# Three-slot units, more dynamic slots at the end, and a band made from a skewed slice, in a convolution with a mixture of experts

## The chip, the cores and the metric

The kernel runs on one core of a Trainium2 chip. A core has five engines with queues of their own: TensorE (PE; its weight loads are shown as PEld), VectorE (DVE), ScalarE (ACT), GpSimd (POOL) and SyncE (SP, which here only issues DMAs). The time is device microseconds of one execution. The kernel before was run 14 times: median 721.24 us, lowest 711.25, highest 727.46. The profile is of one execution of 717.46 us, whose span (first to last instruction) is 715.7 us.

## What is computed

First a depthwise convolution over time with 8 heads, each with 7 taps that went through a softmax; then a mixture of 8 experts with one expert for each token (top 1), in which the expert's output is scaled by the softmax gate and by a sigmoid gate.

```
x: (8, 3584, 192); weight: (8, 7); w_gate, w_output_gate: (192, 8); w1: (8, 192, 1024); w2: (8, 1024, 192)
w = softmax(weight); x_pad = 6 zero rows ahead of each sequence
conv[b, s, h, g] = sum_k w[h, k] * x_pad[b, s + k, h, g]
x = conv.reshape(28672, 192)
logits = x @ w_gate; e_idx = argmax(logits); gate_w = softmax(logits)[e_idx]
eom = sigmoid(x @ w_output_gate)
for e in range(8):
    mask = e_idx == e
    h = relu(x[mask] @ w1[e]); ye = h @ w2[e]
    out[mask] = gate_w[mask] * eom[mask, e] * ye
```

The scale by both gates is applied to the rows before the expert, which the relu lets through, since the scale is positive.

## The kernel before

**Units.** The 28672 tokens are cut into NU = 16 units of 1792 tokens: 16 blocks of BT = 112, a block on the partitions. Two sequences' halves make no difference to what follows, except that a unit at the start of a sequence has zero rows ahead.

**front_a(u)** (line 298, 16 steps, each ended by a `yield`): for each head one matmul pair with the band matrix (line 303) and an eviction into `cv`; then `load_x(u + 2)`; six transposes of `cv` into `tt` (line 317); the logits (line 326) into `lt`; a transpose back (line 335) into `gb`. Evictions go through `evac`, which sends them to ScalarE or VectorE (lines 291 and 293) by `evac_on` or in turn.

**front_b(u)** (line 347, 12 steps) is the routing. Step 1: largest logit and mask. Step 2: counts (line 374), gates. Step 3: four matmuls that give each token its place among those of its expert (lines 396 to 399). Step 4: the destinations `du` and the first permutation matrices `pm`. Steps 5 to 12: for each of eight groups of 224 tokens a permutation by matmul (line 457), eviction into `xs`, and a scatter of row pairs into the DRAM buffer `xcg`, which is sorted by expert (line 475, an indirect DMA of POOL, held in `pend` until `emit_in`). After the first group `plan(u)` computes on VectorE which rows the slots of this unit take: R counts the row pairs that an expert has received, DN those that slots have taken; a slot takes at most TP = 256 pairs (512 rows), and what is left stays for a later slot.

**Slots.** A `Slot` (line 608) is 512 rows of one expert. `slot_load` loads them with two DMA transposes (`xa`, `xb`, lines 586 and 588) and an index load (`xi`, line 590), all on SP; the loads of a unit wait until all its scatters have landed. `first(q2)` is half of the first layer with relu (lines 626 and 633; relu on ScalarE at 646, every fourth on VectorE at 644); `second(q)` is the second layer for 128 rows (line 668), evicted for two quarters together (line 674) into `y`; `emit_out` issues the indirect DMAs into the output (line 495, POOL). From unit U0 = 2 on each unit runs four slots, experts 0 to 3 in even units and 4 to 7 in odd ones; the last unit runs all eight, and then ND = 3 half slots of 256 rows whose expert is chosen at run time by `pick` (the expert with most left), with its weights copied by `w_dyn` into `wd`. A closing loop (line 803) takes full slots as long as rows are left; its count is 0 for these inputs.

**Order.** The order is written out by hand and nothing reorders it. Units 0 and 1 run their fronts first. Then, in the main loop (line 742), unit u has 16 positions, four for each slot (`pos = 4 * k + q`). While the slots of unit u run, the loop puts in between them the 16 steps of `front_a(u + 2)` as `fa`, the last eight steps of `front_b(u + 1)` as `fs` (its scatters, positions 0 to 7), and the first four steps of `front_b(u + 2)` as `fbn` (one at 12, one at 14, two at 15). After position 7 the loads of the next unit are issued (`loads(u + 1)`). `second` runs one slot behind `first`.

**Weights.** All experts' weights stay in SBUF (`wres`), loaded in 32 pieces by POOL: 8 before unit 0, 8 among units 0 and 1, 16 at positions 4 to 19 counted from unit 2.

**Setup.** The band matrix (118 x 112 for each head; one tap per diagonal) is made by VectorE with 14 predicated copies over four heads each (line 142). The gate weights `wg` are loaded on ScalarE's DMA queue, x tiles 0 and 1 on SP.

## Time and profile before

| | |
|---|---|
| median of 14 runs | 721.24 us (711.25 to 727.46) |
| profiled execution | 717.46 us, span 715.7 us |
| mean granted TensorE clock | 0.944 |
| first slot's first matmul | 78.10 us |
| one unit of four slots, from 380.37 to 423.07 | 42.70 us |
| last unit's first dynamic half slot starts | 687.15 us |
| output scatters on POOL | 246 x 994 ns |
| row scatters on POOL | 128 x 1040 ns |
| HBM read, written | 35.92 MB, 43.06 MB |

A profile line for an instruction gives its start in us from the start of the span, its length, engine, source line, operation, output and inputs, and in brackets how long the engine was idle before it and what released it. "issue" is idle time for which the profile shows no cause. Busy TensorE time is not TensorE at its peak; its clock is granted by a throttle and shown as a share of full speed.

### The profile page before, as it was taken

What the parts mean: (1) busy time and instruction counts of PE and PEld (TensorE: products, weight loads), DVE (VectorE), ACT (ScalarE), POOL (GpSimd) and SP (SyncE); (2) the same over time, 40 slices, a digit from 0 to 9 for tenths busy, and PEclk for the clock granted to TensorE, in tenths of its full rate; (3) what the DMA queues carried; (4) which work ended last, traced back from release to release, by engine and by line L of the source; (5) the groups of instructions that cost most, each with busy time, mean ns of one, the idle gap of its engine ahead of it and who ended that gap; (6) DMA issues with size and microseconds to landing.
All of it is one profiled execution on the core that took longest, in us unless ns stands there. A gap on an engine that the chain in (4) does not pass through costs nothing.

```text
span 715.7 us, 13578 instructions
## 1 busy us (share of the span) xinstructions
PE 609.9 (85%) x4544; PEld 368.8 (52%) x4544; DVE 380.0 (53%) x1310; ACT 377.3 (53%) x638; POOL 403.2 (56%) x419
## 2 busy tenths in 40 slices
PE   3998699869797989889799897997989798699883
PEld 1564265535554655546555554654555465365452
DVE  7666657428274573735639275472836539134121
ACT  2777466524654554545455554564555455455442
POOL 1487277746555565455555646565564645655563
PEclk9999899989999999989999999999999899899896
DMA  6989389945163462714536164462715234256310
GB/s 165 208 168 301 89 193 155 228 94 157 55 144 114 97 161 77 168 63 103 148 82 173 67 130 123 89 162 76 174 64 108 66 86 85 79 126 168 114 40 29
DMA packets 162568, 88.13 MB, mean 123 GB/s; under 512 B 116765, under 2 KB 153792, under 8 KB 162496
## 3 DMA queue, kind: packets, MB, share of 16 engines
q1 hardware_dynamic: 131872, 43.92, 27.7%
q0 software_dynamic: 29728, 43.30, 23.3%
q8 instruction: 36, 0.59, 0.3%
q14 instruction: 36, 0.29, 0.1%
q10 hardware_dynamic: 896, 0.03, 0.1%
HBM read 35.92 MB, written 43.06 MB: 110 GB/s over the span
## 4 chain that ended last, share of the span: by engine, by line
PE 64%; issue 11%; DVE 7%; ACT 6%; POOL 5%; DMA 4%; another core or an unknown queue 1%; POOLq 0%; SPq 0%; ACTq 0%; DVEq 0%
PE pyt L668 16%; PE pp L626 13%; PE pf L303 11%; PE pp L633 7%; PE pf L457 6%; PE pf L317 5%; POOL out_dram L495 4%; PE pf L326 4%; ACT ht L646 3%; DVE ht L644 2%; DMA out_dram<-y,oi 2%; ACT cv L291 1%; DVE band L142 1%; PE pf L335 1%
## 5 line engine op out<-in xcount | busy, mean ns | idle before, releaser
L495 POOL DMA_INDIRECT out_dram<-y,oi x246 | 244.5, 994 | 178.1 <-ACT y L674 115.7
L646 ACT ACTIVATE ht<-pp 128x1024 f16<-128x1024 f32 (+1 forms) x189 | 184.8, 1005 | 79.1 <-PE pp L633 36.4
L668 PE MATMUL pyt<-wres,ht 128*128 128x192 f16 x1920 | 194.5, 249 | 1.5 <-issue 1.5
L475 POOL DMA_INDIRECT xcg_sorted<-xs,du x128 | 133.1, 1040 | 110.3 <-ACT xs L291 69.4
L668 PEld LDWEIGHTS <-ht 128*128 128x128 f16 x1968 | 170.5, 99 | 27.6 <-issue 14.4
L303 PE MATMUL pf<-xt,band 118*112 118x384 f32 x256 | 111.0, 529 | 42.7 <-ACT cv L291 27.0
L644 DVE TENSOR_SCALAR ht<-pp 128x1024 f16<-128x1024 f32 (+1 forms) x63 | 75.4, 1197 | 111.3 <-PE pp L626 55.8
L626 PE MATMUL pp<-xa,wres 128*128 128x512 f16 x240 | 98.0, 408 | 12.8 <-ACT ht L646 9.6
L291 ACT CAST xs<-pf 128x388 f16<-128x388 f32 x128 | 62.0, 487 | 73.0 <-PE pf L457 40.1
L674 ACT COPY y<-pyt 128x384 f32<-128x384 f32 x123 | 59.1, 480 | 77.8 <-PE pyt L668 23.4
L626 PE MATMUL pp<-xb,wres 128*128 128x512 f16 x240 | 96.1, 401 | 0.7 <-DMA xb<-xcg_sorted 0.7
L633 PE MATMUL pp<-xb,wres 64*128 64x512 f16 x240 | 77.9, 403 | 0.5 <-ACT ht L646 0.5
L633 PE MATMUL pp<-xa,wres 64*128 64x512 f16 x240 | 78.0, 403 | 0.0
L457 PE MATMUL pf<-xrow,pm 112*128 112x194 f16 x512 | 67.8, 256 | 11.3 <-ACT xs L291 3.2
L626 PEld LDWEIGHTS <-wres 128*128 128x128 f16 x480 | 35.4, 100 | 79.0 <-issue 77.4
L303 PEld LDWEIGHTS pf<-xt,band 118*112 118x112 f32 x256 | 42.8, 188 | 61.5 <-ACT cv L291 29.8
L457 PEld LDWEIGHTS <-pm 112*128 112x128 f16 x512 | 47.0, 101 | 42.1 <-issue 20.9
L293 DVE COPY cv<-pf 112x384 f32<-112x384 f32 x48 | 26.4, 551 | 78.1 <-PE pf L303 72.8
L427 DVE TENSOR_SCALAR pm<-pos,pos 112x256 f16<-112x256 f16 x256 | 62.7, 305 | 0.0
L422 DVE TENSOR_TENSOR xrow<-cv,gs 112x384 f16<-112x384 f32 x121 | 61.9, 549 | 0.0
L317 PE MATMUL pf<-identf,cv 112*128 112x112 f32 x384 | 52.0, 262 | 9.3 <-DVE tt L293 4.4
L291 ACT COPY cv<-pf 112x384 f32<-112x384 f32 x80 | 38.0, 478 | 27.2 <-PE pf L303 21.0
(135 smaller groups left out, 435.9 us busy)
## 6 DMA issues: line engine op xcount, KB each, us to landing
xt<-in_x_dram SPq DMA_DIRECT2D x8, 1344.0 KB
xt<-in_x_dram SPq DMA_DIRECT2D x8, 1260.0 KB
out_dram<-y,oi POOLq DMA_INDIRECT x246
wres<-in_moe_w_dram POOLq DMA_DIRECT2D x8, 384.0 KB
wd<-wres SPq DMA_DIRECT2D x3, 768.0 KB
wres<-in_moe_w_dram POOLq DMA_DIRECT2D x8, 256.0 KB
xcg_sorted<-xs,du POOLq DMA_INDIRECT x128
xcg_sorted<-zrow SPq DMA_DIRECT2D x8, 256.0 KB
```

The costliest lines, as they stand in the source:

```text
L291: nc.scalar.copy(out=o, in_=i)
L303: nc.tensor.matmul(pc[0:BT, 0:NB * GH], band[0:KI, h, :], xt[0:KI, :, h * GH:(h + 1) * GH], start=True, stop=True)
L317: nc.tensor.matmul(pt[:, j * BT:(j + 1) * BT], cvf[0:BT, m * 2 * D + i * 128:m * 2 * D + (i + 1) * 128], identf[0:BT, 0:BT], is_transpose= ...
L427: nc.vector.tensor_scalar(out=pms[i][P, l, :], in0=pos16[P], scalar1=pos[P, l * NG + i:l * NG + i + 1], scalar2=None, op0=ALU.is_equal)
L457: nc.tensor.matmul(ps[:, r * XW:(r + 1) * XW], pm[P, l, r * 128:(r + 1) * 128], xr[P, l * NG + i, :], start=(r == 0 and l == 0), stop=(r = ...
L475: i = nc.gpsimd.indirect_dma_start(out=xcg2, out_offset=bass.IndirectOffsetOnAxis(ap=du[:, i:i + 1], axis=0), in_=xs.rearrange("p r w -> p ...
L495: i = nc.gpsimd.indirect_dma_start(out=out, out_offset=bass.IndirectOffsetOnAxis(ap=oi[:, j:j + 1], axis=0), in_=y[:, j, :], in_offset=Non ...
L626: nc.tensor.matmul(pps[r][:, l, :], w[:, o2:o2 + 128], x, start=(r == 0), stop=(r == 1))
L633: nc.tensor.matmul(pps[r][:, l, :], w[p0:p0 + 64, c:c + 128], x[p0:p0 + 64], start=(r == 1), stop=(r == 0))
L644: nc.vector.tensor_relu(out=ht, in_=pps[r])
L646: nc.scalar.activation(out=ht, in_=pps[r], func=AF.Relu)
L668: nc.tensor.matmul(self.pp[:, o:o + D], self.ht[fc // 2][:, fc % 2, q * 128:(q + 1) * 128], self.w[:, w:w + D], start=(fc == 0 and q % 2 = ...
```

## The change

Six edits, of which the first three belong together.

- Units 4, 6, 8, 10 and 12 run three slots instead of four (`THREE`). Experts are taken in a running order (`nexte`), so that a unit continues where the one before stopped; a run that passes expert 7 is planned in two parts. The last unit still runs all eight, in the running order.
- After the last unit there are six dynamic slots instead of three half ones: two full (512 rows) and four half (256 rows). Their weight copies use buffers of two pools in turn. The last slot of all evicts and scatters each quarter by itself (`end`).
- In the main loop the steps are laid out anew. Short units run `front_a` in 12 positions and only the first step of `fbn` (at 10); the unit after a short one, and unit 2, then run 11 steps of `fs` (positions 0 to 10) and issue the next loads after position 10 instead of 7. Other units run the four steps of `fbn` at 12, 13, 14 and 15. While a short unit scatters rows, `emit_out` holds back four output scatters; unit 14 holds back eight. Before the main loop only one step of `front_b(3)` is run instead of four.
- Weights: 12 pieces before unit 0, four in unit 0, 16 at positions 8 to 23.
- The band: tokens of a block are now in reversed order, so that each head's band is a skewed slice of one line of 229 numbers. Heads 0 and 1 are still made by predicated copies (7, over two heads each); the lines of heads 2 to 7 are written to DRAM by ScalarE's queue and read back with a step of one element per partition. The ids of the tokens (`idu`) follow the reversed order.
- The gate weights are loaded on SP, between x tiles 0 and 1. In unit 0 the transposes are evicted in turn by ScalarE and VectorE; before the main loop `lt` is evicted in two halves by both.

```diff
-    ND = 3
+    DYN = (TP, TP) + (TP // 2,) * 4
+    ND = len(DYN)
...
     xts = {0: load_x(0)}
+    for i, (p0, p1, d0) in enumerate([(0, 128, 0), (0, 64, 128), (64, 128, 0), (0, 128, 64)]):
+        nc.sync.dma_start(wg[p0:p1, i, 0:E], moe_w_gate[d0:d0 + p1 - p0, :])
+        nc.sync.dma_start(wg[p0:p1, i, E:2 * E], moe_w_output_gate[d0:d0 + p1 - p0, :])
     xts[1] = load_x(1)
...
+    HB = 2
+    LW = BT + KI - 1
     band = const.tile([128, H, BT], FP32)
-    nc.vector.memset(band, 0.0)
+    nc.vector.memset(band[:, 0:HB, :], 0.0)
+    wline = const.tile([1, H - HB, LW], FP32)
+    nc.vector.memset(wline, 0.0)
+    wldr = nc.dram_tensor("tap_lines", (H - HB, LW), FP32, kind="Internal").ap()
...
+    nc.scalar.copy(out=wline[:, :, BT - 1:KI], in_=cw[0:1, HB:H, :])
+    nc.scalar.dma_start(wldr, wline)
+    nc.scalar.dma_start(band[0:KI, HB:H, :],
+                        bass.AP(tensor=wldr.tensor, offset=wldr.offset,
+                                ap=[[1, KI], [LW, H - HB], [1, BT]]))
...
-    for h in (0, H // 2):
-        for k in range(KW):
+    for k in range(KW):
+        m = idpu[:, 128 - BT - k:128 - k]
...
+    load_w(12)
...
-    def emit_out():
-        while pout:
+    def emit_out(keep=0):
+        while len(pout) > keep:
...
+    THREE = (4, 6, 8, 10, 12)
+    nexte = [0]
     def plan(u):
         if u < U0:
             return []
-        p = plan_half(u % 2, "a")
-        if u == NU - 1:
-            p += plan_half((u + 1) % 2, "b")
+        n = 3 if u in THREE else 4 if u < NU - 1 else E
+        e0 = nexte[0]
+        nexte[0] = (e0 + n) % E
+        if n == E:
+            p = plan_run(0, E, "a")
+            return p[e0:] + p[:e0]
+        p = plan_run(e0, min(n, E - e0), "a")
+        if e0 + n > E:
+            p += plan_run(0, e0 + n - E, "b")
         return p
...
+            if self.end:
+                nc.scalar.copy(out=self.y[:, q, :], in_=self.pp[:, 0:D])
+                pout.append((self.y, self.oi, q))
...
-    drain(fbn, 4)
+    drain(fbn, 1)
...
+        late, short = u == U0 or u - 1 in THREE, u in THREE
+        last_s = 10 if late else 7
+        if short:
+            before = {0: 1, 2: 1, 4: 1, 6: 1, 8: 1}
+            after = {0: 1, 1: 1, 2: 1, 3: 1, 4: 1, 5: 1, 6: 1, 7: 1, 8: 1, 9: 1, 10: 1}
+        else:
+            before = {0: 1, 2: 1, 4: 1, 6: 1, 8: 1, 9: 1, 10: 1}
+            after = {1: 1, 3: 1, 5: 1, 7: 1, 8: 1, 9: 2, 10: 1, 11: 1}
...
-                if 0 <= 16 * (u - U0) + pos - 4 < 16:
+                if 0 <= 16 * (u - U0) + pos - 8 < 16:
                     load_w(1)
                 if q % 2 == 0:
                     s.first(q // 2)
-                if pos in (0, 2, 4, 6, 8, 10, 12):
-                    evac_on[0] = "act" if pos < 8 else None
-                    drain(fa, 1)
-                if pos == 14:
+                evac_on[0] = "act" if pos < 8 else None
+                drain(fa, before.get(pos, 0))
+                if late and pos == 2:
+                    drain(fs, 1)
+                if not short and pos in (14, 15):
                     drain(fbn, 1)
                 if prev is not None:
                     prev.second(q)
-                    emit_out()
+                    emit_out(8 if u == NU - 2 and pos < 8 else 4 if short and pos < 8 else 0)
...
-                if pos == 12:
-                    drain(fbn, 1)
-                if pos == 15:
-                    drain(fbn, 2)
-                if pos == 7 and u + 1 < NU:
+                if pos == 10 if short else pos in (12, 13):
+                    drain(fbn, 1)
+                if pos == last_s and u + 1 < NU:
                     nxt = loads(u + 1)
                 if u == NU - 1 and q == 3 and k < ND:
-                    todo.append(load_pick())
+                    todo.append(load_pick(DYN[k]))
```

## The prediction

> **What bounds the kernel now.** First the page's busy line and its slices: one engine is nearly full, and only TensorE.
>
> ```profile
> PE 609.9 (85%) x4544; PEld 368.8 (52%) x4544; DVE 380.0 (53%) x1310; ACT 377.3 (53%) x638; POOL 403.2 (56%) x419
> PE   3998699869797989889799897997989798699883
> ```
>
> Then the chain of waits inside one unit, in order of time (start, length, what). One slot's share of it:
>
> ```profile
> 410.75 0.43 PE pp L626 x2
> 411.18 0.54 PE pp L633 x4
> 411.72 0.54 PE pp L626 x2
> 412.64 0.66 PE pyt L668 x8
> ```
>
> The three first rows are half of a slot's first layer (1.51 us), the last is a quarter of its second layer. A full slot is 2 x 1.51 + 4 x 0.66 = 5.66 us of TensorE at full clock. The stretches say what a unit of four slots takes and how its idle time costs twice:
>
> ```profile
> 380.37:423.07 42.70, 38.19 (x292) 23.14 (x290) 24.43 (x80) 23.04 (x37) 23.84 (x24) 0.96 0.47 120
> 404.40:406.90 2.50, 2.50 (x9) 0.54 (x8) 0.00 (x0) 1.38 (x2) 1.89 (x3) 0.50 0.24 77
> 380.40:391.70 11.30, 9.93 (x74) 6.12 (x74) 10.78 (x43) 6.77 (x12) 6.05 (x7) 1.00 0.81 205
> ```
>
> Columns: stretch, length, busy of PE, PEld, DVE, ACT, POOL, granted clock, DMA share, GB/s. The unit from 380.37 to 423.07 has TensorE busy 38.2 of 42.7 us at a mean clock of 0.96. Its clock falls to 0.50 for 2.5 us after a gap. VectorE is full (10.8 of 11.3 us) only in the unit's first quarter. So the middle is TensorE's, and a slot taken away there is worth its TensorE time as long as rows arrive in time. The rows that tell when they do are these: the last row scatter of a unit, the first load that waits for it, and (from the first slot of all, where nothing else hides it) the time from load to matmul.
>
> ```profile
> 407.79 0.98 POOL L475 DMA_INDIRECT xcg_sorted<-xs,du  x1 [0.30 <-issue]
> 410.29 1.14 SPq L586 DMA_TRANSPOSE xa<-xcg_sorted  x1
> 411.62 1.15 SPq L588 DMA_TRANSPOSE xb<-xcg_sorted  x1
> 76.92 1.14 SPq L588 DMA_TRANSPOSE xb<-xcg_sorted  x1
> 79.42 0.59 PE L626 MATMUL pp<-xb,wres 128*128 128x512 f16 x1 [0.73 <-DMA xb<-xcg_sorted]
> ```
>
> Scatter to load 2.50 us, xa to xb issue 1.33 us, xb to its matmul 2.50 us: 6.3 us from the start of the last scatter until the next unit can run. Here the next unit starts at 423.07, 15.3 us after that scatter: 9 us to spare. The change spends this reserve.
>
> At the end there is no front work left; slots follow each other:
>
> ```profile
> 640.68 0.98 POOL L495 DMA_INDIRECT out_dram<-y,oi  x1 [2.02 <-ACT y L674]
> 647.41 0.98 POOL L495 DMA_INDIRECT out_dram<-y,oi  x1 [1.89 <-ACT y L674]
> 675.84 0.38 PE L626 MATMUL pp<-xa,wres 128*128 128x512 f16 x1
> 681.49 0.38 PE L626 MATMUL pp<-xa,wres 128*128 128x512 f16 x1
> ```
>
> Between the same row of two slots lie 6.73 us where they stall (647.41 - 640.68) and 5.65 where they don't. POOL's four output scatters take 4 x 1.29 = 5.2 us of it, so TensorE still leads.
>
> **Part by part. Slots removed.** Units 4, 6, 8, 10 and 12 run three slots: 5 slots less. Each is 5.66 / 0.96 = 5.9 us; bounds 5.65 (no stall goes with it) and 6.73 (the stalled tail row). 5 x 5.9 = -29.5 (-28.3 to -33.7).
>
> **Slots added at the end.** Three half dynamic slots become two full and four half: two full at 6.73 and one half more. Half slots start at 687.15 and 692.27 (5.1 us apart), and half of the next takes 2.19 us (692.27 to 694.46): 4.4 to 5.1, without stall 2 x 0.87 + 1.32 = 3.1. 13.5 + 4.4 = +17.9 (14.4 to 18.6). The extra picks are some fifteen VectorE instructions of about 0.2 us; three more is 9 us of VectorE, busy 8.9 of 30 us there, and five slots pass between a pick and its slot. The weight copies wd (768 KB, three more) ride SP: their issue follows every 5.5 us (653.94, 659.41), faster than a full slot is eaten. Both cost nothing; if the copies fell behind, each half slot would wait 5.5 - 4.4 = 1.1 us. The capacity of all slots, 55 x 256 + 2 x 256 + 4 x 128 = 15104 row pairs, stands against 14598 that the inputs fill, counted per unit and expert; nothing is left over, before or after, so the closing loop does not run.
>
> **Less reserve at unit ends.** Routing of the next unit is left over: after a short unit only its first step is done, so the scatters of the unit that follows end at position 10 instead of 7 (so too in unit 2). From there TensorE has until the next unit 5 x 0.66 + 2 x 1.51 + 0.44 (L335) + about 0.75 (L374 to L399) = 7.5 us. In the short units they end at position 7 of 12, with 2 x 1.51 + 4 x 0.66 + 2 x 0.38 (L317) + 1.64 (L326) + 0.44 = 8.5 us. What has to fit: 0.5 us (ACT's xs, 0.48), POOL's backlog (0 to 3 us; the scatter at 407.79 came 3.3 us after its matmuls, behind two output scatters) and 6.3: 6.8 to 9.8 us. The short units hold back four output scatters, which keeps their backlog low, and position 10 issues none of its own. A full backlog stalls 2.3 and 1.3 us, none stalls nothing. I take 0.4 us, nearer the low end, at 11 ends (five short, five after them, unit 2): +4.4 (0 to 20). What waits behind the loads on SP is the next input tile, now issued ahead of them in these units (some 7 us of transfer, started 8 us earlier; wanted a unit later).
>
> **Denser short units.** 16 front steps in 12 positions instead of 16. VectorE gets three more evictions of 0.55 in the first quarter, but loses the 2 us of routing that now lies at positions 13 to 15 of the unit before. I take 0; if not, it is inside the range above.
>
> **Routing spread out** in the other units (positions 12 to 15, one step each, instead of two at 15). In the unit shown TensorE idled 0.40 us at 383.76 and 0.97 at 391.36 for it. Seven such passages at 0.4: -2.8 (0 to -9.6).
>
> **Weights.** 12 instead of 8 pieces before the first unit; the last 16 four positions later, so eight instead of four fall on unit 3's scatters. Each piece holds POOL 0.6 to 0.96 us (with the gap 1.26). POOL is back to back from 131 to 149 there, its last scatter (146.62) 11.6 us behind its matmuls (135.0); 4 x 1.26 = 5 us more makes 16.6 + 6.3 = 22.9 against the 17.5 to 19 us a unit has left. Against it stands a wait of 8.19 us at 138.27, put down to an unknown queue in a stretch that moves 152 GB/s; it may go or stay. +1 (-8 to +5).
>
> **Prologue.** The first matmul waits for the band, not for x, whose transfer ends before 9 us:
>
> ```profile
> 10.89 0.45 PEld L303 LDWEIGHTS pf<-xt,band 118*112 118x112 f32 x2 [10.89 <-DVE band L142]
> 11.07 0.32 SPq L98 DMA_DIRECT2D xt<-in_x_dram  x1
> 9.00:10.00 1.00, 0.00 (x0) 0.00 (x0) 0.96 (x2) 0.00 (x0) 0.00 (x0) 1.00 0.13 4
> ```
>
> 14 predicated copies (9.5 us) become 7 of half the width (about 2.4). Heads 0 and 1 could start near 10.3, when x is known to have landed; heads 2 to 7 come through two DMAs in a row from 6.1 us on: two round trips of 2.5 to 4 give 11 to 14. The larger memset of the tap lines (1374 elements on one partition, against 896 in 0.81 us) ends before the taps land at 4.33, and the reversed order of tokens inside a block only changes constants. At most 2 us are won (15.59 is where the second four heads waited). But the gate weights now stand on SP ahead of x tile 1, the last behind the band's landing, so that tile's issue moves from 11.07 to 12 to 15, beside twelve weight pieces; it is wanted at 24.2 and took some 7 us alone, 13 if it shares. -0.5 (-2.5 to +3). The last slot evicts each quarter by itself: -0.5.
>
> Sum: -29.5 + 17.9 + 4.4 - 2.8 + 1 - 0.5 - 0.5 = -10.0 us on an execution of 717.46 us (span 715.7). That execution lies 3.8 below the median of 721.24; I take the difference off the median: 711.2 us.
>
> The Trainium skill, page "TensorE: Matmul & The Clock Gate", Part 1, speaks against the change: it says TensorE falls to half clock after an idle window of about 3.4 us and needs another such stretch of work to recover, so short reserves would be paid twice. The trace shows half clock (0.50) already after a gap of 2.40 us at 402.88, and full clock after 0.97. By the page's window stalls of 2.4 us would add nothing. By the trace, 2.4 us at each of 11 ends would add 11 x 1.6 us, and stalls of 0.4 us nothing.
>
> **Rivals.** (a) Forecast, rows arrive about in time: 711, own range 706 to 717. (b) Stalls leave with the slots (-33.7 + 16), routing pays -6, the unknown wait at 138 goes (-4): 721.2 - 27.7, with 4 for ends about 698. For it: TensorE idles 4.5 us a unit; against it: most of this is one ScalarE stall of about 3.6 us a unit, which the change doesn't touch. (c) The gain is used up: ends stall 1.3 us each (14.3 instead of 4.4), 721. For it: POOL's backlog of 3.3 us in the unit shown; against it, the held-back outputs. (d) Slower: the rows come late at all 11 ends by the full 2.3 us of POOL backlog, and the gap drops the clock (2.5 us at 0.50 and 1.5 at 0.76 lose 1.6 us): 11 x 3.9 = 43 instead of 4.4, 750; with the stall alone, 25, 732. It decides from (10.0 + 4.4) / 11 = 1.3 us an end. For it: reserves of 7.5 and 8.5 against needs up to 9.8; against it, the bounds need the worst queue every time. (e) The closing loop runs: each pass would add a load, a weight copy and a slot in series, 15 us or more; the count of rows excludes it.
>
> **Numbers.** (a) 0.52, (b) 0.20, (c) 0.14, (d) 0.14, (e) below 0.01. Half a per cent (3.6 us) is about what a measurement tells from no change: under 717.6 faster, 0.72; between, 0.14; above 724.9 slower, 0.14. The range 699 to 725 leaves out part of (b) and (d).
>
> **What would show it.** Three-slot units near 37 us against 43, the unit after each near 43; first matmuls of units 5, 7, 9, 11, 13 and of 6, 8, 10, 12, 14 waiting on xa or xb less than 1 us; a tail of 16 slot-widths at some 6.7 us. Wrong if those matmuls wait over 1.3 us each with a clock of 0.5 after them, if tile 1 holds back the second unit, or if unit 4 starts several us late behind the weights.

## The result, and the profile after

The changed kernel takes 754.0 us in the median (750.6 to 760.97), the kernel before 720.5 beside it (711.25 to 728.95): ratio 1.0517, 95% interval 1.0483 to 1.055. The ratios here are taken from the fast runs alone, so this one is not the quotient of the two medians (1.0465). It was forecast at 711.2, with a range of 699 to 725. The profiled execution takes 751.69 us and its span is 750.0, against 717.46 and 715.7 before.

First the page's busy lines and slices, then two groups of TensorE with waits that were not there before (last columns: idle before the group, and what ended most of it):

```profile
PE 611.6 (82%) x4432; PEld 365.8 (49%) x4432; DVE 389.3 (52%) x1375; ACT 362.9 (48%) x614; POOL 393.3 (52%) x410
PE   1199877889878989697978889697969799598975
...
L321 PE MATMUL pf<-xt,band 118*112 118x384 f32 x256 | 109.0, 521 | 33.9 <-DMA band<-tap_lines 20.0
...
L344 PE MATMUL pf<-tt,wg 128*32 128x448 f32 x256 | 45.9, 655 | 32.1 <-ACT tt L309 18.0
```

The convolution's group in the kernel before, for comparison:

```profile
L303 PE MATMUL pf<-xt,band 118*112 118x384 f32 x256 | 111.0, 529 | 42.7 <-ACT cv L291 27.0
```

TensorE is busy about as long as before (611.6 against 609.9 us); of the 34.3 us by which the span grew, 32.6 are idle time. The first two slices (37.5 us) are now nearly empty, and one wait there, for the band, is 20.0 us. The second new wait is the logits matmul (L344) on its evictions, 32.1 us of idle time in all, where the logits matmul of the kernel before (L326) had 2.7. The kernel before waited elsewhere: its convolution (L303) idled 27.0 us for ScalarE's evictions.

Stretch by stretch, from the first matmul on xa of one unit to that of the next (a program of the same instructions has the same boundaries):

| stretch | before | after | difference | predicted |
|---|---|---|---|---|
| up to the first slot | 78.1 | 101.8 | +23.7 | -0.5 |
| units 2 and 3 | 86.3 | 94.2 | +7.9 | +1.4 (one end, weights) |
| units 4 to 13 | 429.6 | 416.3 | -13.3 | -28.3 (slots -29.5, ten ends +4.0, routing -2.8) |
| units 14 and 15 | 93.1 | 94.5 | +1.4 | 0 |
| dynamic slots and end | 28.55 | 43.2 | +14.6 | +17.4 (slots +17.9, quarters -0.5) |
| sum | 715.7 | 750.0 | +34.3 | -10.0 |

Of the 44 us between the two sums (+34.3 and -10.0), 24 lie in the prologue, 15 in the ten units and 6.5 in units 2 and 3. The tail was sized about right.

**Prologue.** The timeline of the changed kernel (start, length, engine and line, what was read and written; in brackets the idle time before and what ended it):

```profile
12.22 0.25 ACTq L150 DMA_DIRECT2D band<-tap_lines  x1
...
12.69 5.63 POOL L275 DMA_DIRECT2D wres<-in_moe_w_dram  x8
...
34.32 0.33 SPq L114 DMA_DIRECT2D wg<-n_moe_w_output_gate_dram  x1
34.34 6.82 PE L321 MATMUL pf<-xt,band 118*112 118x384 f32 x12 [19.98 <-DMA band<-tap_lines]
...
34.70 0.43 SPq L99 DMA_DIRECT2D xt<-in_x_dram  x1
```

The write of the tap lines took 5.8 us (6.43 to 12.2), and reading them back 22.1 us (12.22 to 34.3). Heads 0 and 1 were done at 14.4; heads 2 to 7 waited. The last gate weight on SP waited too, 21.0 us, for the landing of the band (the trace shows both loads on the same semaphore), and behind it x tile 1, issued at 34.70 instead of 11.07.

**Units.** Two units of the changed kernel and its tail; columns: stretch, length, busy time of PE, PEld, DVE, ACT, POOL, granted clock, DMA share, GB/s:

```profile
196.03:236.51 40.48, 34.14 (x239) 19.29 (x237) 18.12 (x58) 18.53 (x29) 20.48 (x20) 0.86 0.60 149
236.51:277.83 41.32, 37.91 (x298) 23.05 (x297) 27.55 (x99) 22.98 (x39) 23.19 (x24) 1.00 0.38 104
...
706.84:750.00 43.16, 30.35 (x258) 19.79 (x256) 9.57 (x35) 18.00 (x30) 22.01 (x23) 0.88 0.15 50
```

A three-slot unit takes 40.5 us (mean of the five: 39.6), where 37 was expected, at a mean clock of 0.86. What happens in it, from PE, ACT and DVE:

```profile
219.89 0.60 PE L335 MATMUL pf<-identf,cv 112*128 112x112 f32 x4
220.33 0.83 PE L701 MATMUL pyt<-wres,ht 128*128 128x192 f16 x8
223.70 1.02 ACT L679 ACTIVATE ht<-pp 128x1024 f16<-128x1024 f32 x1 [1.80 <-remote]
225.07 0.53 ACT L309 COPY tt<-pf 128x448 f32<-128x448 f32 x1 [0.35 <-remote]
225.65 3.21 PE L344 MATMUL pf<-tt,wg 128*32 128x448 f32 x14 [4.50 <-ACT tt L309]
230.02 0.62 DVE L311 COPY tt<-pf 128x448 f32<-128x448 f32 x1 [11.02 <-PE pf L344]
230.70 1.70 PE L344 MATMUL pf<-tt,wg 128*32 128x448 f32 x2 [1.85 <-DVE tt L311]
```

The last transposes (L335) end at 220.5, but VectorE evicts them only at 230.02, after 11.02 us of idleness, and ScalarE evicts the ones before (ended at 219.3) at 225.07, behind an eviction that itself came after 1.80 us of idleness. So the logits matmul waits 4.50 and 1.85 us and runs at half clock (here 4.9 us instead of 1.64). All five short units show the first wait (4.03 to 4.53), four the second at 1.71 to 1.85 and unit 10 at 0.84. The old loop had a wait of this kind in each of units 4 to 13 too, of 2.4 to 3.6 us, most of them before the convolution; in unit 11 it came in two pieces, 1.55 and 1.97. Over units 4 to 13 TensorE's busy time fell from 383.3 to 360.9 us, and its idle time rose from 46.4 to 55.3.

### The profile page after: what moved, and what is told of

The parts are those of the page before. It is cut to its first block, busy times and chain, and to the rows that moved or that the text cites. A ratio compares the mean times of both kernels' runs of the same rounds, so it can differ in the third digit from the quotient of the medians.

```text
span 750.0 us, 13275 instructions
## 1 busy us (share of the span) xinstructions
PE 611.6 (82%) x4432; PEld 365.8 (49%) x4432; DVE 389.3 (52%) x1375; ACT 362.9 (48%) x614; POOL 393.3 (52%) x410
## 4 chain that ended last, share of the span: by engine, by line
PE 56%; issue 8%; DVE 7%; ACT 4%; another core or an unknown queue 4%; DMA 3%; POOL 3%; SPq 0%; POOLq 0%; ACTq 0%; DVEq 0%
PE pyt L701 16%; PE pp L659 13%; PE pp L666 7%; PE pf L321 6%; PE pf L344 4%; PE pf L479 4%; PE pf L335 4%; ACT ht L679 4%; DVE ht L677 2%; DMA xb<-xcg_sorted 2%; DMA xcg_sorted<-xs,du 1%; POOL xcg_sorted L497 1%; DVE xrow L444 1%; POOL out_dram L517 1%
## 5 line engine op out<-in xcount | busy, mean ns | idle before, releaser
L517 POOL DMA_INDIRECT out_dram<-y,oi x236 | 234.7, 994 | 163.1 <-ACT y L710 100.8
L679 ACT ACTIVATE ht<-pp 128x1024 f16<-128x1024 f32 (+1 forms) x183 | 177.7, 997 | 88.8 <-PE pp L666 43.9
L701 PE MATMUL pyt<-wres,ht 128*128 128x192 f16 x1760 | 181.5, 251 | 0.8 <-issue 0.8
L701 PEld LDWEIGHTS <-ht 128*128 128x128 f16 x1888 | 166.1, 100 | 30.4 <-issue 13.2
L659 PE MATMUL pp<-xa,wres 128*128 128x512 f16 x220 | 88.0, 400 | 14.7 <-issue 7.4
L659 PE MATMUL pp<-xb,wres 128*128 128x512 f16 x220 | 86.7, 394 | 2.3 <-DMA xb<-xcg_sorted 2.3
L311 DVE COPY tt<-pf 128x448 f32<-128x448 f32 x48 | 29.6, 617 | 101.5 <-PE pf L344 42.7
L666 PE MATMUL pp<-xb,wres 64*128 64x512 f16 x220 | 70.9, 397 | 7.6 <-ACT ht L679 7.4
L479 PEld LDWEIGHTS <-pm 112*128 112x128 f16 x512 | 45.1, 98 | 55.4 <-issue 37.0
L344 PE MATMUL pf<-tt,wg 128*32 128x448 f32 x256 | 45.9, 655 | 32.1 <-ACT tt L309 18.0
L666 PE MATMUL pp<-xa,wres 64*128 64x512 f16 x220 | 71.1, 398 | 0.0
L659 PEld LDWEIGHTS <-wres 128*128 128x128 f16 x440 | 32.1, 99 | 70.0 <-issue 68.1
L335 PE MATMUL pf<-identf,cv 112*128 112x112 f32 x384 | 54.8, 275 | 7.2 <-issue 2.6
```

The costliest lines, as they stand in the source:

```text
L335: nc.tensor.matmul(pt[:, j * BT:(j + 1) * BT], cvf[0:BT, m * 2 * D + i * 128:m * 2 * D + (i + 1) * 128], identf[0:BT, 0:BT], is_transpose= ...
L344: nc.tensor.matmul(pl[32 * g:32 * g + 32, 0:4 * BT], wg[:, (g // 2) * 2 + i, :], tt[:, g // 2 + i, (g % 2) * 4 * BT:(g % 2 + 1) * 4 * BT], ...
L479: nc.tensor.matmul(ps[:, r * XW:(r + 1) * XW], pm[P, l, r * 128:(r + 1) * 128], xr[P, l * NG + i, :], start=(r == 0 and l == 0), stop=(r = ...
L517: i = nc.gpsimd.indirect_dma_start(out=out, out_offset=bass.IndirectOffsetOnAxis(ap=oi[:, j:j + 1], axis=0), in_=y[:, j, :], in_offset=Non ...
L659: nc.tensor.matmul(pps[r][:, l, :], w[:, o2:o2 + 128], x, start=(r == 0), stop=(r == 1))
L666: nc.tensor.matmul(pps[r][:, l, :], w[p0:p0 + 64, c:c + 128], x[p0:p0 + 64], start=(r == 1), stop=(r == 0))
```

## The experiments

The runs met chips of two speeds: the first chip and two others run the kernel before in 720 to 728 us, two more ("quick" below; the first twelve runs are theirs) in 624.2 to 625.0. So a run is compared only with the kernel before on its own chip, by its ratio. A single operation takes the same on both (ScalarE's ht eviction 1.02 us); what the quick chips lack is the wait once a unit. A four-slot unit of the old loop there takes 36.67 us, with TensorE busy 35.96 at a clock of 1.00 (from f4 below; the kernel before itself was not profiled on such a chip).

### The changed kernel on a quick chip (after_again)

> The changed kernel as it is, beside the three others and on their chip: the chip of the last four ran the kernel before in 624.6 us against 720.5 on the first. Theory: the sum of the terms seen there (first slot +21, loop and tail +8 as in the old-band run) gives before + 27 to 30, ratio 1.04 to 1.05. Rival: the time is lost in the stalls seen only on the first chip; then the ratio falls to 1.03 or less.

Measured: 656.1 us, ratio 1.0508 (1.0443 to 1.0573). First slot at 101.19, ten units 360.9 us, tail 38.1. The loss is as large on a chip without the once-a-unit wait, so that wait is not its main cause.

### The band's landing: e1, e2, e3, e4

e1_band_split reads the band in two parts:

```diff
-    nc.scalar.dma_start(band[0:KI, HB:H, :],
-                        bass.AP(tensor=wldr.tensor, offset=wldr.offset,
-                                ap=[[1, KI], [LW, H - HB], [1, BT]]))
+    for q0, q1 in ((0, BT), (BT, KI)):
+        nc.scalar.dma_start(band[q0:q1, HB:H, :],
+                            bass.AP(tensor=wldr.tensor, offset=wldr.offset + q0,
+                                    ap=[[1, q1 - q0], [LW, H - HB], [1, BT]]))
```

> Theory A: the band read is slow because its 118 rows are spread over few of the 16 DMA engines (it took 22 us for 317 KB, from 12.2 to 34.3). Read as 112 rows and 6 rows it should land by about 15 to 17 us, heads 2 to 7 of unit 0 start there instead of at 34.3, and the time falls by 17 to 19 us, to about 736 (731 to 740). Theory B: the read is slow because twelve weight pieces issued from 12.7 us on share the engines with it. Then the split changes little: landing after 28 us, time 748 to 756.

e2_weights_late takes the twelve weight pieces away from the setup:

```diff
-    load_w(12)
...
-            if u == 0 and n > 4 and n % 2:
+            if u < U0 and n > 4:
                 load_w(1)
```

> The twelve weight pieces leave the setup; eight go out beside unit 0's row scatters and eight beside unit 1's. Theory B (contention): the band lands by 16 us and the time falls to about 736 (731 to 742). Theory A (few engines): the band still lands after 28 us and the time is 746 to 756. If both act, the landing lies between, 19 to 28 us.

Measured: split 645.4 us, ratio 1.0308 (1.0264 to 1.0351); weights late 648.1, 1.0369 (1.0333 to 1.0404). Without weights beside it the band still lands only at 21.9. The stretch from 12 to 22 us of that run, in the columns used above, and from its timeline the matmul that ends the wait:

```profile
12.00:22.00 10.00, 2.73 (x5) 0.90 (x4) 1.49 (x9) 0.96 (x2) 0.31 (x1) 1.00 0.14 33
```

```profile
21.89 6.25 PE L320 MATMUL pf<-xt,band 118*112 118x384 f32 x12 [7.27 <-DMA band<-tap_lines]
```

The read, issued at 11.88, has the queues almost to itself and takes 10.0 us. The sixteen DMA engines are busy by 0.14, which is a little over two of them, and move 33 GB/s. In the changed kernel the same ten us show a share of 0.92. Split, with all weights beside it, the band lands at 16.1, as the timeline of e1 shows:

```profile
16.13 5.70 PE L322 MATMUL pf<-xt,band 118*112 118x384 f32 x12 [1.70 <-DMA band<-tap_lines]
...
23.95 8.83 SPq L100 DMA_DIRECT2D xt<-in_x_dram  x1
...
34.05 4.15 PE L322 MATMUL pf<-xt,band 118*112 118x384 f32 x6 [6.29 <-DMA xt<-in_x_dram]
```

Both theories hold: 118 rows use few engines (10.0 us where the 112 + 6 rows take 4), and with the weights beside it the same read takes 22.1 us. That the two multiply is not shown: split and without weights (g3 below) the read takes 3.7 us instead of 4.0. In e1 it was issued at 12.12, 0.5 us ahead of the first weight piece. The Trainium skill, page "DMA: Bandwidth & Descriptors", section "Why a DMA increments its semaphore by 16 and not by 1", says a transfer uses the largest number of engines up to 16 that divides the slowest dimension of both its sides. For 118 rows that is 2 and for 112 it is 16; the share of 0.14 and the gain of the split agree. The time fell by less than expected: e1 lies 10.7 us below the changed kernel (after_again) instead of 17 to 19. Unit 1 now starts only at 34.05, where it waits for x tile 1, issued at 16.4 among the weight pieces.

e3_old_band puts back the 14 predicated copies and the old token order inside a block; gate weights on SP and the twelve early pieces stay.

```diff
-    nc.scalar.copy(out=wline[:, :, BT - 1:KI], in_=cw[0:1, HB:H, :])
...
-    for k in range(KW):
-        m = idpu[:, 128 - BT - k:128 - k]
+    for h in (0, H // 2):
+        for k in range(KW):
+            m = idpu[:, k:k + BT]
...
```

> The new kernel with the old band (14 predicated copies, no tap lines in memory, old order of tokens inside a block), everything else new. If the first slot's delay (78.1 to 101.8) is the band's alone: first slot at 77 to 81, time 754.0 - 23.7 = 730 (727 to 734). Rival: the gate weights on SP and the twelve weight pieces cost by themselves: first slot at 85 or later, time 737 or more.

e4_new_band_alone is the kernel before with the new band and the gate weights on SP, the same lines as in the change.

> The kernel before with the new band and the gate weights on SP; its unit loop, eight weight pieces at the start and three half dynamic slots are the old ones. If the loss of the prologue is a plain delay that nothing later wins back: 720.5 + 20 to 24 = 741 to 745. Theory B with eight weight pieces instead of twelve: some two thirds of it, 734 to 738. Rival: the delay is absorbed by reserve in the old loop: below 728.

Measured: e3 633.2 us, ratio 1.0127 (1.0094 to 1.016), first slot at 79.92: 22.9 us below the changed kernel (after_again). e4 643.3 us, 1.028 (1.0234 to 1.0326), 18.7 us above the kernel before; the band lands at 31.8 with eight weight pieces beside it. So the band costs some 19 to 23 us, by itself and in either loop. In e4 it is a little less than the 20 to 24 us that I expected from the delay of the first slot.

### Mending the new band: f2, f4, g3

f2_split_x1_first is e1 with x tile 1 ahead of the gate weights; f4_old_loop_split_x1 is e4 with both; g3_split_weights_late is e1 and e2 together.

```diff
 # f2, f4
     xts = {0: load_x(0)}
+    xts[1] = load_x(1)
     for i, (p0, p1, d0) in enumerate(...):
         nc.sync.dma_start(wg[...], ...)
-    xts[1] = load_x(1)
```

> The changed kernel with the band read split (112 rows and 6) and x tile 1 issued ahead of the gate weights. Theory: after the split, unit 1 waits for x tile 1, which stands on SP behind gate weights that wait for the band; issued early, unit 1's convolution starts by 27 instead of 34 and the first slot at 79 to 83 instead of 91.6; time 10 us below the split alone, before + 8 to 11. Rival: x tile 1 is slow because of the twelve weight pieces, not of its place; then the first slot stays at 88 or later and the time within 4 us of the split alone (before + 17 to 21).

> The kernel before (loop, eight weight pieces, tail) with the new band read in two parts and x tile 1 ahead of the gate weights. Theory: with the band's landing mended nothing of the new prologue is slow, and what is left is its small gain: 0 to 4 us below the kernel before. Rival: the memory round trip of the taps still ends later than the 14 copies did, 15.5: 2 to 6 us above it.

> The changed kernel, with the band read split and the twelve weight pieces moved out of the setup (eight beside unit 0's row scatters, eight beside unit 1's). Each alone brought the first slot from 101.2 to 91.6 (split) and 94.2 (weights). Theory: the two causes multiply (few engines, each of them shared), so together the band lands at 14 to 16, x tile 1 follows at once and alone, and the first slot starts at 80 to 83: ratio 1.015 to 1.022. Rival: the causes overlap, and x tile 1 behind the band keeps the first slot at 88 or later: ratio 1.027 or more.

Measured: f2 644.1 us, 1.028 (1.0201 to 1.036), first slot 89.5. f4 633.4 us, 1.0119 (1.0063 to 1.0174), first slot 89.8. g3 642.4 us, 1.0296 (1.0259 to 1.0332), first slot 88.1. All three missed their theories; the rivals' numbers hold for f2 and g3, and f4 lies above its rival's 2 to 6 us too. In f2 and f4 the tap lines' write ends 1.1 to 1.2 us later than in e1, and the band's read, issued at 13.22 and 13.34 instead of 12.12, now stands behind the first weight pieces (from 12.64 and 12.52 on) as well as beside x tile 1. It takes 8.9 and 9.1 us and lands at 22.1 and 22.5 instead of 16.1; how much of this is the tile's and how much the weights' was not separated. In g3 the band lands at 15.8 and the front work is done by 77.6, but the first slot then waits for its rows:

```profile
71.85 0.96 POOL L276 DMA_DIRECT2D wres<-in_moe_w_dram  x1 [1.57 <-DMA wres<-in_moe_w_dram]
...
88.07 0.59 PE L659 MATMUL pp<-xa,wres 128*128 128x512 f16 x1 [10.45 <-DMA xa<-xcg_sorted]
```

The weight pieces now stand on POOL between unit 1's row scatters, the last of which ends at 83.5. Each of the three repairs brought the band or the first slot sooner and made something else wait; none reached the 79.9 of the old band.

### Slots and tail: f3, g1, g2

f3_no_short gives every unit four slots and the tail three half slots; the rest is the changed kernel.

```diff
-    DYN = (TP, TP) + (TP // 2,) * 4
+    DYN = (TP // 2,) * 3
...
-    THREE = (4, 6, 8, 10, 12)
+    THREE = ()
```

> The changed kernel with four slots in every unit and three half dynamic slots, all else (slow band, early routing layout, weights) as it is. Theory: a slot taken out of a unit is worth only 2 to 3 us, five of them 10 to 14, against 14 us for the longer tail; so this is 0 to 4 us faster than the changed kernel run beside it. Rival (the prediction's terms: slots -29.5, ends +4.4, tail +17.9): this is 7 us or more slower.

Measured: 645.8 us, ratio 1.0315 (1.0257 to 1.0372): 10.3 us below the changed kernel, more than the 0 to 4 us of the theory. Its tail is 26.3 us instead of 38.1, its ten units take 362.7 instead of 360.9. So on a quick chip five removed slots won 1.9 us in all. The stretches show why. Two units of f3_no_short:

```profile
257.53:293.99 36.46, 36.13 (x294) 22.83 (x292) 23.35 (x78) 23.43 (x38) 24.70 (x24) 1.00 0.58 136
293.99:329.94 35.95, 35.94 (x293) 22.73 (x292) 24.16 (x78) 22.91 (x37) 24.21 (x24) 1.00 0.52 137
```

A short unit and the next of the changed kernel on such a chip, and two us of the second:

```profile
255.37:286.07 30.70, 29.72 (x238) 18.79 (x236) 20.48 (x66) 18.66 (x31) 18.02 (x18) 1.00 0.50 130
286.07:327.32 41.25, 38.97 (x297) 23.80 (x298) 27.53 (x97) 22.96 (x38) 26.73 (x27) 0.96 0.50 130
...
288.00:290.00 2.00, 2.00 (x7) 0.79 (x8) 0.00 (x0) 1.27 (x2) 1.39 (x3) 0.56 0.61 135
```

Its timeline at the seam of the two units:

```profile
286.07 0.39 PE L659 MATMUL pp<-xa,wres 128*128 128x512 f16 x1 [0.86 <-ACT ex L379]
...
287.62 0.38 PE L659 MATMUL pp<-xb,wres 128*128 128x512 f16 x1 [1.15 <-DMA xb<-xcg_sorted]
```

The short unit is 5.5 us shorter, as counted, and the unit after it 5 us longer. At its start TensorE waits 0.86 and 1.15 us for rows, then runs at half clock from 288.24 to 291.65; it also does the routing steps that the short unit left over. (The first wait carries ScalarE's name, but what that matmul reads is xa, whose load was issued at 283.25, 2.8 us before.)

Units 14 and 15 take 71.0 us in f3_no_short and 71.8 in the changed kernel, but 78.7 in the old loop (f4). There unit 14's last row scatter starts 7.6 us behind its matmuls, TensorE waits 2.10 and 0.43 us for the rows of unit 15, and the mean clock of unit 15 is 0.93. In f3_no_short, where unit 14 holds back eight output scatters, it starts 1.1 us behind them and TensorE does not wait. That the held-back outputs are the reason was not tried alone.

g1_rows_early ends the row steps of the short units two positions sooner:

```diff
-        last_s = 10 if late else 7
+        last_s = 10 if late else 5 if short else 7
...
-                    drain(fs, 1)
+                    drain(fs, 2 if short and pos in (1, 3) else 1)
```

> The changed kernel, with the eight row steps of each three-slot unit at positions 0 to 5 (two at 1 and 3) instead of 0 to 7. Theory: on this chip the worth of a short unit is lost at its end, where TensorE waits 2.0 us for xa and xb (1.9 to 2.0 at four of the five ends) and then runs 3 us at half clock; with the last row scatter 3 us earlier the wait goes, each pair of units falls from 71.9 to 68.5 to 69.5, and the time by 11 to 17 us below the changed kernel's ratio: ratio to before 1.025 to 1.035. Rival: TensorE's work itself does not shrink as counted, or the wait is a load's and not a row's: pairs stay above 71, ratio 1.045 to 1.055.

g2_u2_four_steps does four routing steps of unit 3 ahead of unit 2, instead of one, so that unit 2's rows end at position 7.

```diff
-    drain(fbn, 1)
+    drain(fbn, 4)
     fill[0] = None
...
-        late, short = u == U0 or u - 1 in THREE, u in THREE
+        late, short = u - 1 in THREE, u in THREE
```

> The changed kernel, with unit 3's routing done four steps ahead of unit 2 (as in the kernel before) instead of one, so unit 2's rows end at position 7. Theory: units 2 and 3 take 81.5 us on this chip against 74.4 in the old loop because unit 2's rows come 3.05 us late and the start is cold; with the four steps back the two take 74 to 77, the first slot starts 0 to 3 us later, and the time falls by 3 to 6 us: ratio 1.041 to 1.046. Rival: the steps only move from one side of the first slot to the other: ratio 1.048 to 1.053.

Measured: g1 645.8 us, ratio 1.0358 (1.0322 to 1.0394); g2 651.3 us, 1.0431 (1.0379 to 1.0482). g2 is as its theory had it, and g1 is at the edge of its range (1.025 to 1.035; pairs of 69.7 us where 68.5 to 69.5 were expected). In g1 the five pairs take 348.5 us instead of 360.9, and the ends of the short units no longer wait:

```profile
253.87:284.50 30.63, 29.87 (x238) 18.88 (x237) 19.95 (x62) 18.34 (x29) 18.93 (x19) 1.00 0.53 136
284.50:322.78 38.28, 37.16 (x299) 23.02 (x297) 28.62 (x101) 23.00 (x39) 25.90 (x26) 1.00 0.51 135
```

In g2 units 2 and 3 take 74.6 us instead of 81.5, and the first slot starts at 101.98 instead of 101.19. In g1 a slot taken out is worth (362.7 - 348.5) / 5 = 2.8 us; the five win 14.2 and the longer tail costs 11.8. The rest of the slot's 5.66 us went partly into idle time: over the ten units TensorE is busy 24.6 us less than in f3_no_short (335.9 against 360.5) and idle 10.3 us more (12.6 against 2.3).

### What is left of the change: h1 and k1

h1_old_band_no_short_u2 keeps the routing spread over positions 12 to 15, the eight output scatters held back in unit 14, the quarter evictions, the early weights and the gate weights on SP. It takes back the rest (the edits of e3, f3 and g2 together).

> What is left of the change without the parts that cost: old band, four slots in every unit, three half dynamic slots, four routing steps ahead of unit 2; kept are the routing spread over positions 12 to 15, quarter evictions of the last slot, the early weights and the gate weights on SP. Theory: only the spread routing remains, 0.45 us a unit (36.2 against 36.67 us), so 2 to 6 us below the kernel before: ratio 0.990 to 0.997. Rival: early weights cost the first units more than that: 1.000 to 1.008.

Measured: 618.1 us against 624.2, ratio 0.9907 (0.988 to 0.9934), first slot at 80.23. The ten units take 364.9 us; the old loop with the mended band (f4) took 366.7. So the spread routing is the smaller part of the gain: units 14 and 15 and the tail together take 97.4 us against 102.7 in f4.

k1_old_band_rows_early_u2 keeps the short units and mends the rest (e3, g1 and g2 together). It met a chip as slow as the first.

> The change with its three losses mended: old band, four routing steps ahead of unit 2, rows of the short units at positions 0 to 5; short units and the long tail are kept. Theory: ends mended, five slots are worth 16 us (348.5 against 364.9 for ten units) and the tail costs 12.2 (38.2 against 26.0), so this is 3 to 5 us below the version without short units (ratio 0.9907): 0.982 to 0.987. Rival: the gains of the parts do not add, as the units' ends and POOL's queue are shared: 0.990 or above.

Measured: 729.7 us against 727.7, ratio 1.0029 (0.9989 to 1.0068). That is no difference that can be told. The rival's number holds, but not shown is its reason (shared ends and POOL's queue), since this chip has the once-a-unit waits, which the theory's sum left out. Its first slot starts at 82.62, its tail is 45.1, and its ten units take 428.2 us, no fewer than the old loop's 429.6 on the first chip. Its logits matmuls wait again, 3.85 to 4.69 us in the five short units. Whether the parts add up on a quick chip was not tried.

### The once-a-unit wait on a slow chip: k2 and four runs repeated

k2_logits_later puts the logits matmul of the short units at position 10 and its transposes at 11.

```diff
-            after = {0: 1, 1: 1, 2: 1, 3: 1, 4: 1, 5: 1, 6: 1, 7: 1, 8: 1, 9: 1, 10: 1}
+            after = {0: 1, 1: 1, 2: 1, 3: 1, 4: 1, 5: 1, 6: 1, 7: 1, 8: 1, 10: 1, 11: 1}
...
-                if pos == 10 if short else pos in (12, 13):
+                if pos == 11 if short else pos in (12, 13):
```

> The changed kernel, with the logits matmul of the short units one position later (10 instead of 9, its transposes 11). On the first chip it waited 4.0 to 4.5 us for ScalarE's eviction and 1.8 for VectorE's, in every short unit. Theory: there the later place hides 3 us or more of each, so on a chip with such waits the short units go from 39.6 to 36 to 37.5 and the ratio from 1.0517 to 1.03 to 1.035. On the chip of the last twelve runs, where these waits are under 0.1 us, theory and rival (a wait that moves with the matmul) both give the changed kernel's own 1.051 within 0.007.

Measured: 748.5 us against 727.7, ratio 1.0302 (1.0237 to 1.0368). The ratio is the theory's, the cause is not: the short units take 38.5 to 40.0 us, not 36 to 37.5. The wait moved. In unit 4 it went to the next matmul, as the timeline shows:

```profile
225.91 1.71 PE L344 MATMUL pf<-tt,wg 128*32 128x448 f32 x16
...
233.96 1.10 PE L357 MATMUL pf<-identf,lt 128*112 128x128 f32 x4 [5.57 <-ACT lt L309]
```

The logits matmul no longer waits, but the transposes of its result (L357) wait 5.57 us for ScalarE's eviction. In the other four short units the wait comes as pieces of 0.9 to 2.2 us, most before matmuls of the slots. TensorE's idle time in the five is 5.1 to 8.2 us a unit, against 6.0 to 7.0 in the changed kernel. The changed kernel's ratio itself was 1.0364 on the next slow chip, so 1.0302 against 1.0517 says little.

Four kernels once more, unchanged (after_2, f3_no_short_2, h1_old_band_no_short_u2_2, g1_rows_early_2), on a slow chip:

> The changed kernel beside the three others, in the hope of a chip like the first (before: 720.5 and 727.7 there, 624.2 to 625.0 on the other). Its ratio was 1.0517 on the first chip and 1.0508 on the other; 1.045 to 1.055 again.

> The changed kernel with four slots in every unit and three half dynamic slots. On the other chip this was 10 us faster than the changed kernel. Theory: on the first chip, too, the slots saved (13 us of the ten units in its profile) are worth no more than the longer tail costs (14.6): within 5 us of the changed kernel, or below it. Rival: on the first chip the slots pay and this is 6 us or more slower than the changed kernel.

> The version that beat both kernels on the other chip (0.9907): old band, no short units, four routing steps ahead of unit 2. Theory: its gain is the spread routing, which does not depend on the chip: 0.985 to 0.997. Rival: on a chip where evictions are delayed once a unit it gains nothing: 0.998 to 1.006.

> The changed kernel with the rows of the short units at positions 0 to 5. On the other chip 11 us below the changed kernel, since the waits for xa and xb at the short units' ends went. On the first chip these waits were not there (under 0.3 us in its profile), so theory: within 4 us of the changed kernel there. Rival: 8 us or more below it.

Measured (before: 724.3 us): the changed kernel 748.4, ratio 1.0364 (1.03 to 1.0428); f3_no_short 759.8, 1.0478 (1.0414 to 1.0542); h1 737.3, 1.0116 (1.0018 to 1.0215); g1 760.0, 1.0533 (1.0467 to 1.0599). The changed kernel lies below the 1.045 to 1.055 expected of it. f3_no_short went to the rival's side: there the short units do pay (11.4 us less than without them). g1 met neither theory nor rival, which had it level with the changed kernel or faster: it is 11.6 us slower. h1 lies beyond its rival's 1.006, but its four runs spread from 726.9 to 738.6 us, and whether it is slower than the kernel before stays unclear. A part of g1's loss lies where its instructions are the changed kernel's own: unit 2 took 50.16 us against 45.60. So differences of a few us between two kernels on such a chip need not be the edit's, and no version found here was shown to beat the kernel before on every chip.

## Why the prediction was wrong, step by step

- **Prologue, -0.5 (range -2.5 to +3): wrong, and the largest error.** The failed step is "two round trips of 2.5 to 4 give 11 to 14". The write took 5.8 us and the read 22.1. Nothing in the profile before shows a transfer of 118 rows (the kernel's own `load_x` reads its 118 rows as 112 and 6), and I priced it by the latency of other transfers instead of bounding it by the width it could use. The same step named the twelve weight pieces beside x tile 1, but not beside the band. e1 and e2 showed both halves, few engines and shared ones; e3 showed that the delay of the first slot is the band's.
- **"At most 2 us are won":** e3 starts its first slot at 79.9 and h1 at 80.2, without the new band, so nothing was to be won there; f2, f4 and g3 did not get below 88.
- **Slots removed, -29.5: the count was right, the worth was not.** The short unit is 5.5 us shorter on the quick chip, but the pair only 0.4. With the ends mended a slot is worth 2.8 us there. On the first chip ten units won 13.3 us: TensorE's busy time fell by 22.3 and its idle time rose by 9.0. The rise lies in the short units (32.0 us of idle time against 23.7 in the same five before): it is the once-a-unit wait, which I took as untouched ("one ScalarE stall of about 3.6 us a unit, which the change doesn't touch"). In a short unit it took 6.0 us on average, and the clock with it.
- **Less reserve at unit ends, +4.4 (0 to 20): right mechanism, mis-sized, and on the other chips.** On the first chip unit 2's end waited (2.49 and 0.60 us at 151.46 and 152.44) and unit 14's start (0.45 and 1.07); the other ends did not show it. On the quick chip the short units' ends wait 1.8 to 2.0 us instead of 0.4 and lose clock on top; g1 gave 12.4 us back. Unit 2's end costs 6.9 us there (g2). The reserve was right: in unit 6 the next unit could have run 8.6 us after the last permutation matmul (8.5 reckoned). What had to fit was larger, 11.0 us instead of 6.8 to 9.8: the last scatter (280.68) started 4.07 us after its matmuls, behind two output scatters although four were held back, and 6.94 us passed from it to the first matmul on xb at 287.62 (6.3 reckoned; the matmul on xa, 0.4 us, lies in between). The term of 0.4 also left out the clock. On the first chip the same scatter stands as far behind its matmuls, but 13 to 15 us before the next unit, since the once-a-unit wait comes after it.
- **The clock.** I weighed the idle window of 3.4 us that the Trainium skill names ("TensorE: Matmul & The Clock Gate", Part 1) against a row at 2.40, as if the length of one gap decided. The traces show something else: in every one the granted clock changes only at multiples of one step of 3.41 us, and what counts is the idle time inside a step, in one piece or several. In after_again TensorE is busy 1.40 us of the step from 284.83 to 288.24, which holds the waits of 0.86 and 1.15 us, and the next step is at half clock. In all 20 profiles together half clock followed each of the 149 full-clock steps with 1.95 us or more of idle time, 36 of the 64 steps with 1.62 to 1.95, and none of the 3289 with less. So the step has the window's length, but one that is about half idle is enough. A stall near that size costs another 1.7 us (half a step, an estimate) or nothing, by how it lies in the steps.
- **Slots added, +17.9 (14.4 to 18.6): about right.** The tail grew by 14.6 us on the first chip, by 11.8 to 14.1 on the quick one (against f3 and f4): the low end or below it. The two full slots took 5.9 and 6.2 us on the first chip and 5.65 each on the quick one, without a stall.
- **Routing spread, -2.8 (0 to -9.6):** on a quick chip -4.0 over ten units (366.7 in f4 against 362.7 in f3). On the slow chip h1, which has it, came out at 1.0116, unclear.
- **Units 14 and 15, no term:** +1.4 us on the first chip, but 6.9 us less than the old loop (71.8 against 78.7 in f4) on the quick one. The forecast named the held-back outputs only for the short units' ends.
- **Weights, +1 (-8 to +5):** not separated from unit 2's late rows. The wait of 8.19 us at 138.27 is VectorE's, a late eviction; TensorE waited 4.41 us for it (at 147.17). In the changed kernel TensorE waits 2.47 us before 131.80 for such an eviction, and 2.49 us before 151.46 for rows.
- **Last slot by quarters, -0.5:** inside the tail's error; not tried alone.
- **Rivals.** (d) had given 750, close to the result, by rows late at all eleven ends. The profile does not show that: most ends of the first chip did not wait, so the nearness of 750 is chance. (c) is nearest in kind for the quick chip: the gain is used up at the ends. No rival had the band; the bound of +3 excluded it.

Open: what delays the evictions once a unit on the slow chips. It is there in the old loop and in the new one, at different instructions; moving the logits matmul moved it; the quick chips run the same program without it.

## What to carry to other kernels

Price a new transfer by its shape: count rows against the engines they can use, and add whatever is issued beside it. Where no row of that shape exists, the upper bound is its bytes at the rate of the few engines that it can use (33 GB/s here), with whatever shares them on top, not a round trip. A piece of work taken out of a stage is worth its time only as far as the next stage's inputs are ready that much sooner; compute scatter, load and clock recovery at the shortened end before booking the gain. Work moved to the tail, where nothing overlaps it, is paid in full.

## What the runs showed of the hardware

- 118 rows by 6 by 448 B took 10.0 us with 0.14 of the DMA engines busy and little beside it (e2), 22.1 us with twelve weight pieces; split into 112 and 6 rows 4.0 us when issued just ahead of the pieces (e1), 8.9 us behind the first of them and beside an x tile (f2).
- The same program took 624 to 625 us on two chips and 720 to 728 on three. The matmuls and evictions looked at take equally long; on the three ScalarE and VectorE start some evictions late, once a unit (5.8 and 9.5 us after their transposes in the unit shown), and TensorE's clock falls after it.
- The granted clock changed only in steps of 3.41 us. Half clock followed every step with 1.95 us or more of idle time, in one piece or several, and none with less than 1.62 us.
